# Two attention and SwiGLU layers in split fp32: which queue issues the first loads and the values' copies, the order of the normalization, of the transposes and of a product's parts, and which engine makes the weights' low parts

## The chip, the cores and the metric

The kernel runs on one core of one Trainium2 chip. The time is the device time of the slowest core, here the only one, in microseconds (us); the median of several runs counts. The engines of the core have these names in what follows: TensorE (PE in the profile; PEld is its weight load), VectorE (DVE), ScalarE (ACT), GpSimd (POOL) and SyncE (SP). SyncE computes nothing here; it only issues DMA copies. Each engine works through its own instructions in the order in which the program has them, and copies that an engine issues stand in that same order.

## What is computed

The input x has 2048 rows and 448 columns. All is in 32-bit floating point.

```python
def _A_ref(x, wq, wk, wv, wo):            # 16 heads of 28, one shared key and value head
    q = (x @ wq).reshape(B, S, H, Dh).transpose(0, 2, 1, 3)
    k = x @ wk
    v = x @ wv
    scores = jnp.einsum("bhqd,bkd->bhqk", q, k) * (Dh ** -0.5)
    p = _softmax(scores, axis=-1)
    o = jnp.einsum("bhqk,bkd->bhqd", p, v)
    return o.transpose(0, 2, 1, 3).reshape(B, S, H * Dh) @ wo

def _B_ref(x, w_gate, w_up, w_down):      # inner width 1792
    return (_silu(x @ w_gate) * (x @ w_up)) @ w_down

x = x + _A_ref(_layernorm(x), ...)
x = x + _B_ref(_layernorm(x), ...)
x = x + _A_ref(_layernorm(x), ...)
x = x + _B_ref(_layernorm(x), ...)
```

## The kernel before

**Number format.** TensorE takes its operands in a reduced form of fp32 (fp32r). A value is therefore held as a high part and a low part, both fp32r, and a product is high times high, high times low and low times high. A weight's high part is a cast (`wh`) and its low part the difference (`wl`); the normalized x has the parts `xh` and `xl`.

**Tiling.** The 2048 rows are four chunks c = 0 to 3 of 512 rows, each of four tiles of 128. The attention's projection of a chunk has four blocks of 128 output columns, written q(c,m) here. They are made in the order of `TURN`, m = 3, 0, 1, 2: block 3 holds the last 64 columns of q, then v and k; blocks 0 to 2 hold the other columns of q. A block is one `product_T` (L258): 11 matmuls of 128x512, for each of the four pieces k of 128 input columns. The fourth piece has only 64 columns, and its low part lies in the lower half of `xh[3]`, so it needs two matmuls where the others need three.

**What stands ahead of a chunk's blocks.** `norm_steps` (L211) gives the steps of the normalization: the statistics of four tiles on VectorE (L217, L218), `rstd` of all four on GpSimd (L222, L223), and for each tile the subtraction and scaling on VectorE (L230) and a copy of its last columns on GpSimd (L231). `flip` (L242) then turns the result: for each k four transposes on TensorE into one of the four banks `LOW` (L248), the high part by ScalarE (L252) and the low part by VectorE (L254, for k = 3 L256). The flip of chunk c+1 stands in `project` (L402) ahead of the last block of chunk c, that is of q(c,2).

**What a block leaves.** `q` (L422) empties the block's bank with ScalarE, for m = 3 and for the very first blocks straight into the high part (L439), otherwise as fp32 (L442), which GpSimd then splits (L140, L141). Both parts go into one of a ring of three buffers (`halves`, named q2) and from there by a copy to DRAM, `qd` (L445). A buffer is taken again only when its copy has landed. Block 3 also sends k into the stack of the keys `kstack` (four copies, issued by L132), and transposes v on VectorE (L454) and copies it into `vsb` (four copies, L456). `stack(i)` (L314) reads `qd` back into the stack of queries of a group of four heads, in four copies, `high(i)` (L323) reads the high parts alone into `qhigh`, and `diagonal` (four copies, L132) fills `kdiag`. With these two, `quick_steps` computes a bound for the softmax, which goes into the stack by four copies named `down` (L132). A list `waiting` lets one of diagonal, high and stack out behind each block.

**The queues.** All copies of the program are issued by SyncE, in program order. The framework gives every copy one of eight semaphores, in turn over all copies of the program, whichever queue they are on; a copy is not issued before the previous one on its semaphore has landed.

**The start.** The prelude (L731 to L764) issues the loads of the four tiles of chunk 0, then the first layer's weights (`load_wqkv`, L171: block 3's columns with v and k, then the first 256 of q), then the rows of chunks 1 to 3. ScalarE casts the first weights and VectorE makes their low parts (L193, L194; `parts`). GpSimd sets `kstack`, `vsb`, `qhigh`, `kdiag` and the three `qstack` to zero (from L747 to L759) and makes chunk 1's `rstd` behind them. `plan` says behind which block the normalization of the chunks 1 to 3 runs in layer 0. In layer 1 the normalized chunks come out of the feed-forward of layer 0 and `plan` is not used for them.

**Behind the projections.** The scores (L511), the exponentials (L518), the product with the values (L546), the output projection (L503), and the feed-forward (its products by `product_T`, L641 for the way down) take nearly all of the time. A second, slower form of the whole (`full`) stands behind a condition and isn't run on these inputs. The feed-forward uses `product_T` as well, and the order of its eleven matmuls is the same there.

## Time and profile before

| what | us |
|---|---|
| three runs | 2102.55, 2101.77, 2100.86 |
| their median | 2101.77 |
| profiled execution, its own time | 2104.14 |
| its span, first to last instruction | 2102.1 |

The stretches of the profiled execution, by busy time in us; the granted TensorE clock is a share of full speed, and the DMA share that of the core's 16 DMA engines:

| stretch (us) | what runs | TensorE | VectorE | ScalarE | GpSimd | clock | DMA share |
|---|---|---|---|---|---|---|---|
| 0 to 100 | start, projections of layer 0, first scores | 74.80 of 100 | 41.66 | 38.60 | 41.88 | 0.93 | 0.57 |
| 100 to 1016 | scores and feed-forward of layer 0 | 915.73 of 916 | 231.45 | 546.88 | 149.87 | 1.00 | 0.16 |
| 1016 to 1130 | projections of layer 1 | 100.42 of 114 | 51.81 | 33.94 | 31.68 | 0.94 | 0.36 |
| 1130 to 2102 | scores and feed-forward of layer 1 | 963.07 of 972 | 248.92 | 561.72 | 142.12 | 1.00 | 0.15 |

How the rows below are read. A row of a timeline has the start in us, the duration in us, the engine and the line of the program, the operation, the output and input by their names in the program, how many such instructions stand together, and in square brackets the idle time of that engine ahead of it with what ended it. SPq is SyncE's queue; its rows are issues of copies, and a row's duration there runs from the first issue of the group to the last's end. A row of waits has the engine's line, then what it waited for, then the total in us, how often, and the longest. A row of a grouped view has the operation with its shapes, then busy us in total and mean ns of one, then the idle time before. "LN <- DMA x" is a wait for the landing of a copy into x.

### The profile page before, as it was taken

The numbers are of one execution on the slowest core, as the hardware profiler recorded it, in microseconds if no ns is written. First come the engines' busy times: TensorE is split into PE (matmuls) and PEld (weight loads), VectorE is DVE, ScalarE is ACT, GpSimd is POOL, SyncE is SP. The second block draws the span as 40 slices with busy tenths as digits, with TensorE's granted clock in tenths as the row PEclk, the third lists the DMA queues.
The fourth block names the chain that finished last, engine by engine and source line by source line (L and its number), as shares of the span: only waits on it lengthen the run. The fifth ranks groups of instructions, "written<-read, shape, count | busy, mean of one in ns | idle before, by whom it ended". The sixth has DMA issues, their size and how long they took to land.

```text
span 2102.1 us, 28049 instructions
## 1 busy us (share of the span) xinstructions
PE 2054.0 (98%) x11073; PEld 1371.4 (65%) x11073; DVE 573.8 (27%) x1150; ACT 1181.1 (56%) x1600; POOL 365.5 (17%) x386
## 2 busy tenths in 40 slices
PE   7899999999999999999989999999999999999998
PEld 5544544545458888888775445455454588888887
DVE  6110131211105333333551112212111163333333
ACT  2599799798982111111127997988979621111111
POOL 5202010103201111111231111011212111111100
PEclk9999999999999999999999999999999999999999
DMA  6413122122200111110142222121322000111001
GB/s 183 137 30 70 30 54 49 35 53 60 49 6 20 29 29 29 29 29 10 32 130 79 55 51 50 29 56 29 70 43 48 25 10 21 29 29 30 29 1 72
DMA packets 98540, 97.21 MB, mean 46 GB/s; under 512 B 28992, under 2 KB 68320, under 8 KB 98400
## 3 DMA queue, kind: packets, MB, share of 16 engines
q1 hardware_dynamic: 98400, 95.34, 18.3%
q8 instruction: 89, 1.46, 0.3%
q14 instruction: 51, 0.42, 0.1%
HBM read 73.53 MB, written 18.61 MB: 44 GB/s over the span
## 4 chain that ended last, share of the span: by engine, by line
PE 91%; DMA 3%; DVE 2%; SPq 2%; POOL 1%; ACT 1%; issue 0%; ACTq 0%; POOLq 0%; DVEq 0%
PE bank L266 27%; PE bank L546 22%; PE pair L511 16%; PE bank L641 12%; PE bank L511 7%; PE pair L503 3%; DMA qd<-q 1%; PE pair L338 1%; PE bank L503 1%; DMA o<-rd 1%; PE bank L248 1%; DVE stats L217 1%; DVE xres L647 0%; SPq L132 0%; SPq L456 0%
## 5 line engine op out<-in xcount | busy, mean ns | idle before, releaser
L518 ACT ACTIVATE pt<-pair 128x1024 f32<-128x1024 f32 x768 | 763.5, 1029 | 0.7 <-PE pair L511 0.7
L546 PE MATMUL bank<-pt,vsb 128*32 128x512 f32 x4096 | 492.1, 598 | 0.0
L511 PE MATMUL pair<-qstack,kstack 128*128 128x512 f32 x1536 | 399.7, 395 | 1.2 <-ACT q L442 1.2
L518 ACT ACTIVATE pt<-bank 128x512 f32<-128x512 f32 x512 | 308.2, 602 | 90.8 <-PE bank L511 84.2
L266 PE MATMUL bank<-xh,wgh 128*128 128x512 f32 x896 | 349.1, 390 | 0.3
L266 PE MATMUL bank<-xh,wgl 128*128 128x512 f32 x896 | 348.5, 389 | 0.0
L511 PEld LDWEIGHTS pair<-qstack,kstack 128*128 128x128 f32 x1536 | 286.4, 188 | 62.3 <-ACT q L442 2.1
L695 ACT ACTIVATE sg<-bank 128x512 f32<-128x512 f32 x112 | 67.2, 600 | 372.4 <-PE bank L266 358.6
L641 PE MATMUL bank<-wdh,h 128*128 128x448 f32 x896 | 273.0, 365 | 0.0
L546 PEld LDWEIGHTS bank<-pt,vsb 128*32 128x32 f32 x4096 | 107.2, 109 | 245.0 <-issue 243.9
L266 PE MATMUL bank<-xl,wgh 128*128 128x512 f32 x672 | 261.5, 389 | 0.0
L697 ACT CAST h<-sg 128x512 fp32r<-128x512 f32 x112 | 69.5, 620 | 319.9 <-DVE sg L696 319.9
L511 PE MATMUL bank<-qstack,kstack 128*128 128x512 f32 x512 | 218.8, 427 | 2.7 <-ACT pt L518 2.7
L511 PEld LDWEIGHTS bank<-qstack,kstack 128*128 128x128 f32 x512 | 96.0, 187 | 156.1 <-ACT pt L518 144.4
L579 POOL TENSOR_TENSOR o<-o 128x512 f32<-128x512 f32 x32 | 41.2, 1287 | 898.7 <-DMA o<-rd 712.3
L266 PEld LDWEIGHTS bank<-xh,wgl 128*128 128x128 f32 x896 | 168.2, 188 | 35.0
L266 PEld LDWEIGHTS bank<-xh,wgh 128*128 128x128 f32 x896 | 168.2, 188 | 34.8 <-issue 1.7
L696 DVE TENSOR_TENSOR sg<-bank,sg 128x512 f32<-128x512 f32 x112 | 77.5, 692 | 414.9 <-PE bank L266 398.8
L641 PEld LDWEIGHTS bank<-wdh,h 128*128 128x128 f32 x896 | 168.1, 188 | 14.8
L641 PE MATMUL bank<-wdl,h 128*128 128x448 f32 x448 | 162.5, 363 | 0.0
L558 DVE COPY o<-bank 128x512 f32<-128x512 f32 x32 | 22.1, 692 | 456.1 <-PE bank L546 456.1
L266 PEld LDWEIGHTS bank<-xl,wgh 128*128 128x128 f32 x672 | 126.1, 188 | 23.5
(98 smaller groups left out, 1507.7 us busy)
## 6 DMA issues: line engine op xcount, KB each, us to landing
qstack<-qd SPq DMA_DIRECT2D x128, 224.0 KB
qd<-q SPq DMA_DIRECT2D x24, 512.0 KB
o<-rd SPq DMA_DIRECT2D x32, 256.0 KB
qhigh<-qd SPq DMA_DIRECT2D x128, 56.0 KB
wdr<-in_B_w_down_dram SPq DMA_DIRECT2D x28, 224.0 KB
wr<-in_B_w_gate_dram SPq DMA_DIRECT2D x28, 192.0 KB
wr<-in_B_w_up_dram SPq DMA_DIRECT2D x28, 192.0 KB
out_dram<-xres SPq DMA_DIRECT2D x16, 224.0 KB
```

The source lines that it names most:

```text
L217: nc.vector.bn_stats(stats[:, 4 * c + t, :], xres[:, 4 * c + t, :])
L266: nc.tensor.matmul(po, a, b, start=(i == 0), stop=(i == len(seq) - 1))
L503: nc.tensor.matmul(po[:, 0:D], a[:, g, ts_], b[:, g, :], start=(g + z == 0), stop=(g == NG - 1 and z == 2))
L511: nc.tensor.matmul(sp[:, e, :], kt_[:, P * kt : P * kt + P], qts[i % 3][:, j, :], start=True, stop=True)
L518: nc.scalar.activation(pt[:, 0 : len(which), :], sp[:, 0 : len(which), :], AF.Exp, scale=SCALE)
L546: nc.tensor.matmul(accs[i][32 * j : 32 * j + 32, :], vsb[:, kt, :], pts.pop((i, (kt, j))), start=(kt == 0), stop=(kt == NT - 1), skip_grou ...
L558: nc.vector.tensor_copy(oraw, accs.pop(i))
L579: nc.gpsimd.tensor_tensor(rb, oraw, rb, ALU.mult)
L641: nc.tensor.matmul(po, a[:, ts_], b, start=(fc == fs[0] and z == 0), stop=(fc == fs[-1] and z == 2))
L695: nc.scalar.activation(sg, pg[0], AF.Silu)
L696: nc.vector.tensor_tensor(sg, pg[1], sg, ALU.mult)
L697: nc.scalar.copy(hh, sg)
```

## The change

- The first layer's loads of wv, wk and the first 256 columns of wq are issued by ScalarE's queue; the remaining columns of wq stay on SyncE (`rows3` takes the engine).
- The subtraction that gives the first weights' low parts runs on GpSimd. The second pair of weight parts is made ahead of the memsets of `kdiag`, `qhigh` and `qstack`, not behind them, and the identity matrix is made ahead of the weights' loads.
- Normalization: chunk 0's `rstd` is made in two halves, the first as soon as the statistics of two tiles are there. The statistics and `rstd` of chunk 1 run in the prelude, and its scaling behind the first block. The statistics of chunks 2 and 3 come one block later than before, their scaling where it was (`plan`). The loads of chunks 1 to 3 are issued ahead of chunk 0's statistics.
- `flip` takes its four banks first, and issues the 16 transposes so that tiles 0 and 1 of all four k come first, then tiles 2 and 3; the copies and subtractions follow all transposes.
- `product_T` multiplies the four high-by-high pairs first, then three high-by-low pairs, then four low-by-high pairs. This holds for the feed-forward too.
- The copies of the values into `vsb` are issued by ScalarE's queue, after the next block's bank has been emptied (`later`), not by SyncE behind the keys. `diagonal` enters `waiting` a little earlier in the same block and is issued by ScalarE in layer 0.

```diff
-    def rows3(dst, src):
+    def rows3(dst, src, eng=None):
         n = src.shape[1]
-        nc.sync.dma_start(dst[:, 0:3], src[0:384, :].rearrange("(k p) n -> p k n", p=P))
-        nc.sync.dma_start(dst[:, 3], src[384:448, :][None].to_broadcast([2, 64, n]))
+        eng = eng or nc.sync
+        eng.dma_start(dst[:, 0:3], src[0:384, :].rearrange("(k p) n -> p k n", p=P))
+        eng.dma_start(dst[:, 3], src[384:448, :][None].to_broadcast([2, 64, n]))
...
-                rows3(r[:, :, 192 : 192 + DH], wv)
-                rows3(r[:, :, 224 : 224 + DH], wk)
+                rows3(r[:, :, 192 : 192 + DH], wv, nc.scalar if first else None)
+                rows3(r[:, :, 224 : 224 + DH], wk, nc.scalar if first else None)
             else:
-                rows3(r, wq[:, 0:256])
+                rows3(r, wq[:, 0:256], nc.scalar if first else None)
...
-                nc.vector.tensor_tensor(wl[:, :, zs], r, wh[:, :, zs], ALU.subtract)
+                nc.gpsimd.tensor_tensor(wl[:, :, zs], r, wh[:, :, zs], ALU.subtract)
...
-        def scale():
+        def scale(ts=slice(0, 4)):
...
+        if c == 0:
+            fs = [lambda t=t: stat(t) for t in range(4)]
+            fs[1:2] = [fs[1], lambda: scale(slice(0, 2))]
+            fs += [lambda: scale(slice(2, 4))] + [lambda t=t: apply(t) for t in range(4)]
+            got["first"] = fs
...
-        for k in ks:
-            pt = place if place is not None else bank(LOW)[1]
-            for t in range(4):
-                nc.tensor.transpose(pt[:, P * t : P * t + P], got["x"][:, t, P * k : P * k + P], ident)
+        pts = {k: place if place is not None else bank(LOW)[1] for k in ks}
+        order = [(k, t) for k in ks for t in range(4)]
+        if len(pts) == 4:
+            order.sort(key=lambda o: o[1] // 2)
+        for k, t in order:
+            nc.tensor.transpose(pts[k][:, P * t : P * t + P], got["x"][:, t, P * k : P * k + P], ident)
+        for k, pt in pts.items():
...
-        for k in range(3):
-            seq += [(a_h[k], xh[:, k, :]), (a_h[k], xl[:, k, :]), (a_l[k], xh[:, k, :])]
-        seq += [(a_h[3], xh[:, 3, :]), (a_l[3], xh[:, 3, :])]
+        for a, b, n in ((a_h, xh, 4), (a_h, xl, 3), (a_l, xh, 4)):
+            seq += [(a[k], b[:, k, :]) for k in range(n)]
...
         def diagonal(self):
             for j in range(4):
-                dma(kd[32 * j : 32 * j + DH, j, :], kt_[0:DH, 0:64])
+                eng = nc.sync if self.layer else nc.scalar
+                eng.dma_start(kd[32 * j : 32 * j + DH, j, :].bitcast(F32), kt_[0:DH, 0:64].bitcast(F32))
...
+            while self.later:
+                self.values(*self.later.pop())
...
-            for u in range(4):
-                nc.sync.dma_start(
+            self.later.append((c, vt))
+
+        def values(self, c, vt):
+            for u in range(4):
+                nc.scalar.dma_start(
...
-    fs, got = norm_steps(0)
-    for f in fs[:4]:
-        f()
+    make_identity(nc, ident)
     parts, at.w = load_wqkv(xb.enter_context(tc.tile_pool(name="wqkv0", bufs=1)), True)
-    make_identity(nc, ident)
-    for f in fs[4:]:
-        f()
-    at.norms[0] = got
...
+    _, got = norm_steps(0)
+    for f in got["first"]:
+        f()
     parts[0]()
-    at.turned(0)
+    flip(got, at.X[0])
...
-    for t in [*qms, *([kd] if kd is not None else []), *qts]:
+    parts[1]()
+    for t in [*([kd] if kd is not None else []), *qms, *qts]:
         nc.gpsimd.memset(t.bitcast(F32), 0.0)
-    parts[1]()
     for c in range(1, NC):
         fs, got = norm_steps(c)
-        at.plan.setdefault((max(0, 4 * c - 6), 1), []).extend(fs[:5])
-        at.plan[4 * c - 3 - (c > 1), 1] = fs[5:] + [lambda c=c, got=got: at.norms.__setitem__(c, got)]
+        if c == 1:
+            for f in fs[:5]:
+                f()
+            at.plan[0, 1] = fs[5:]
+        else:
+            at.plan[4 * c - 5, 1] = fs[:5]
+            at.plan[4 * c - 4, 1] = fs[5:]
+        at.norms[c] = got
```

More of the change, by code (lines that the diff above doesn't have):

```diff
@@ L213, in norm_steps @@
         got = {}
-        cs = slice(4 * c, 4 * c + 4)
         def stat(t):
@@ L218, in stat @@
             nc.vector.bn_aggr(mv[:, 4 * c + t, :], stats[:, 4 * c + t, :])
-        def scale():
-            rstd = pers.tile([P, 4], F32, name="rstd", bufs=2)
-            nc.gpsimd.tensor_scalar(rstd, mv[:, cs, 1], 1.0, EPS, ALU.mult, ALU.add)
-            nc.gpsimd.tensor_tensor(rstd, rstd, halfn, ALU.pow)
-            got["r"] = rstd
+        def scale(ts=slice(0, 4)):
+            if "r" not in got:
+                got["r"] = pers.tile([P, 4], F32, name="rstd", bufs=2)
+            v = mv[:, 4 * c + ts.start : 4 * c + ts.stop, 1]
+            nc.gpsimd.tensor_scalar(got["r"][:, ts], v, 1.0, EPS, ALU.mult, ALU.add)
+            nc.gpsimd.tensor_tensor(got["r"][:, ts], got["r"][:, ts], halfn[:, ts], ALU.pow)
         def apply(t):
@@ L279, in __init__ @@
             self.order = [(c, m) for c in range(NC) for m in TURN]
-            self.seen = 0
+            self.seen, self.later = 0, []
             self.steps, self.places = [], []
@@ L449, in q @@
                 return
+            if c == 0 and not full:
+                self.waiting.append(self.diagonal)
             for z in range(2):
@@ L459, in q @@
                 )
-            if c == 0 and not full:
-                self.waiting.append(self.diagonal)
         def open(self):
```

## The prediction, made before the changed kernel ran

> **What bounds the kernel now.** I read the page first, then TensorE's waits, then the chain of waits and SyncE's queue in the two stretches where TensorE waits.

> ```profile
> span 2102.1 us, 28049 instructions
> PE 2054.0 (98%) x11073; PEld 1371.4 (65%) x11073; DVE 573.8 (27%) x1150; ACT 1181.1 (56%) x1600; POOL 365.5 (17%) x386
> ...
> PE bank L248 <- ACT q L442: 15.2, 4, 5.2
> PE bank L248 <- DVE xn L230: 13.6, 3, 9.9
> ```

> TensorE is busy 98%, so almost nothing can be won or lost in scores and feed-forward. Its idle time (us in total, times, longest) lies in the projections: 15.2 us before transposes (L248) whose bank ScalarE has not yet emptied, 13.6 before transposes whose x is not yet normalized (9.9 of it the start). The change works on just these. The chain through the first projections shows what the 15.2 us are:

> ```profile
> 51.63 6.99 DMA qd<-q
> ...
> 58.72 0.59 ACT q L442
> ...
> 60.01 4.74 DMA qd<-q
> ...
> 78.51 2.14 DMA kstack<-q
> ```

> The copy qd(1,1) left SyncE at 51.63 and landed at 58.62; that freed the buffer into which ScalarE empties q(2,0). qd(1,2) left at 60.01 and landed at 64.75, which freed q(2,1)'s. The last two banks of flip(3) wait for these. So this stretch runs at the pace at which SyncE gets qd(1,1) and qd(1,2) out. The queue, and what it waits for:

> ```profile
> 44.15 2.70 SPq L456 DMA_DIRECT2D vsb<-sg  x4
> 46.89 1.90 SPq L323 DMA_DIRECT2D qhigh<-qd  x4
> ...
> 49.33 2.21 SPq L314 DMA_DIRECT2D qstack<-qd  x4
> 51.63 0.38 SPq L445 DMA_DIRECT2D qd<-q  x1
> 52.07 2.98 SPq L314 DMA_DIRECT2D qstack<-qd  x4
> 55.58 3.55 SPq L132 DMA_DIRECT2D qstack<-down  x4
> 60.01 2.01 SPq L445 DMA_DIRECT2D qd<-q  x2
> ...
> SPq L445 <- DMA qstack<-qd: 1.7, 2, 0.9
> ```

> The last row is the key to this change: qd(1,2), whose data is ready, waits 0.9 us for an unrelated copy, the first of stack 2. The two share a semaphore: eight go round over all copies, and a copy is issued only when the last one on its semaphore has landed.

> **Part 1: the start, +2.1 us.** Two subtractions of 128x1024 leave VectorE (1.23) for GpSimd, ahead of memsets and of chunk 1's rstd.

> ```profile
> 17.53 1.23 DVE L194 TENSOR_TENSOR wl<-wq,wh 128x1024 fp32r<-128x1024 f32 x1 [0.88 <-ACT wh L193]
> ...
> 11.83 1.04 ACT L193 CAST wh<-wr 128x1024 fp32r<-128x1024 f32 x1 [9.62 <-DMA wr<-in_A_wk_dram]
> 34.26 0.59 ACT L442 COPY q<-bank 128x512 f32<-128x512 f32 x1 [5.29 <-PE bank L266]
> ...
> L141 POOL TENSOR_TENSOR wl<-wr,wh 128x1024 fp32r<-128x1024 f32 x2 | 4.8, 2397 | 0.2
> ...
> 11.35 1.81 POOL L751 MEMSET kstack<- 128x2048 f32 x1
> 13.86 0.99 POOL L759 MEMSET qhigh<- 128x512 f32 x2
> 15.05 5.31 POOL L759 MEMSET qstack<- 128x2048 f32 x3
> 23.38 0.20 POOL L222 TENSOR_SCALAR rstd<-mv 128x4 f32<-128x4 f32 x1 [3.02 <-DVE mv L218]
> 23.66 1.02 POOL L223 TENSOR_TENSOR rstd<-rstd,halfn 128x4 f32<-128x4 f32 x1
> 24.71 1.78 DVE L230 TENSOR_SCALAR xn<-xres,mv,rstd 128x448 f32<-128x448 f32 x4 [0.70 <-POOL rstd L223]
> 25.28 2.91 PE L248 MATMUL bank<-ident,xn 128*128 128x128 f32 x16 [1.64 <-DVE xn L230]
> 30.06 0.50 PE L266 MATMUL bank<-xh,wh 128*128 128x512 f32 x1 [1.87 <-DVE xl L254]
> ```

> I leave the first weight cast at 11.83: its loads leave earlier on ScalarE, but each waits for a piece of x on its semaphore, and the last (wq's tail) for all of chunk 1 of x, with the cast behind it on the queue. GpSimd then runs without a gap: cast end 12.87, subtraction 2.40 to 15.3, memsets of kstack to vsb (11.35 to 13.86) 2.51 to 17.8, second subtraction to 20.2, the other memsets (13.86 to 20.36) 6.50 to 26.7, rstd (23.38 to 24.68) 1.30 to 28.0. VectorE normalizes chunk 1 until 29.8 (24.71 before). Behind that stands q(0,0)'s low part, 0.69, to 30.5; its bank is the third of flip(1), and in the new order 12 of the 16 transposes come behind it. At the slow pace of 0.27 (below; TensorE idles some 4 us) they end at 33.8, where q(0,2) starts instead of 30.06. That product ran at half clock (30.06 to 34.26); now at 11 x 0.23 = 2.5 it ends at 36.3: +2.1. Bounds: -1.9 (loads landing two us earlier, transposes at 0.12) to +4 (loads two us later). Hidden under this: the kdiag and values copies on ScalarE that hold q(0,1)'s emptying, and chunk 0's earlier normalization; without that cover flip(1)'s last bank would wait for them until about 28.

> **Part 2: SyncE up to qd(1,1), -0.5 us in each layer.** The values' four copies, 2.70 us (44.15), go to ScalarE. Counted from the end of q(0,2) (34.26), qd(1,1) left at 17.4. Now, by the built program's semaphores: qd(0,2) leaves at 2.7; stack 0's last copy waits until that has landed (4.74, to 7.45); qd(1,3) waits for stack 0's first, about 7.9, where the old one went at 5.5; then kstack 3.56, qhigh 1.90, qd(1,0), stack 1 2.21: qd(1,1) at about 16.9. Of 2.70 some 2.2 are lost to landings. Bounds -2.7 (no wait binds) to +2.

> **Part 3: qd(1,2) behind the values of chunk 2, +4.75 us in each layer.** Now qd(1,2) shares its semaphore with the third values copy of chunk 2, and the second and third "down" copies, ahead of it on SyncE, with the first two. These leave ScalarE only after it has emptied q(2,0), which itself waits for qd(1,1). From that landing: emptying 0.69, first copy's issue 0.68, landing 2.14 (taken from kstack's row, likewise SBUF to SBUF) = 3.5; three down copies at 0.89 = 6.15; then qd(1,2). Before, it left 60.01 - 58.62 = 1.4 after it. Difference 4.75, all of it TensorE's idle time before flip(3)'s last bank. Layer 1 has the same chain:

> ```profile
> 1090.39 0.39 SPq L445 DMA_DIRECT2D qd<-q  x1
> 1090.82 3.06 SPq L314 DMA_DIRECT2D qstack<-qd  x4
> ...
> 1098.59 1.64 SPq L445 DMA_DIRECT2D qd<-q  x2
> 1103.90 1.09 PE L248 MATMUL bank<-ident,xn 128*128 128x128 f32 x4 [5.25 <-ACT q L442]
> ```

> The landing of the small copies under load is not in the trace: 1.2 gives +3.8, qd's loaded 6.99 gives +9.6; I take 2.14, the nearest kind. [...]

> **Part 4: the transposes' order, +0.7 us in each layer.** Of flip(3) only the last 4 transposes came after the wait; sorted by pairs of tiles it is 10.

> ```profile
> 41.78 1.91 PE L248 MATMUL bank<-ident,xn 128*128 128x128 f32 x16
> 65.58 1.09 PE L248 MATMUL bank<-ident,xn 128*128 128x128 f32 x4 [5.10 <-ACT q L442]
> ```

> 1.91/16 is 0.12, after a long idle 1.09/4 is 0.27. [...]

> **Part 5: the hand-over to the scores, +1.15 and +1.45 us.** The last kstack copy of (3,3), which frees q(3,2)'s buffer, now waits for qd(3,3)'s landing.

> ```profile
> 80.24 0.39 PE L511 MATMUL bank<-qstack,kstack 128*128 128x512 f32 x1
> 81.39 0.97 PE L511 MATMUL pair<-qstack,kstack 128*128 128x512 f32 x3 [0.76 <-ACT q L442]
> ...
> 1119.86 0.39 PE L511 MATMUL bank<-qstack,kstack 128*128 128x512 f32 x1
> 1120.70 1.67 PE L511 MATMUL pair<-qstack,kstack 128*128 128x512 f32 x6 [0.45 <-ACT q L442]
> ```

> From q(3,3)'s end: qd after 1.4, landed +4.74, copy 0.86, landed +2.14, emptying 0.65: 9.8. Before, the pair ran 8.65 (layer 0) and 8.35 (layer 1) after that end (the pair at 81.39 and 1120.70; q(3,3) ended three products of 2.5 ahead of the first scores, 80.24 and 1119.86). Bounds 0 to 2.

> **Part 6: high parts first, +1.1 us in layer 1.** The fourth matmul now needs xh[3], whose lower half VectorE writes last.

> ```profile
> 1025.22 0.50 PE L266 MATMUL bank<-xh,wh 128*128 128x512 f32 x1 [0.94 <-DVE xl L254]
> ...
> 1026.40 0.69 DVE L256 TENSOR_TENSOR xh<-bank,xh 64x512 fp32r<-64x512 f32 x1
> ```

> It runs at 1027.12, eight more at 0.23 end the product's turn at 1028.9 instead of 1027.8. Bounds 0 to 1.2. In layer 0 the same wait lies under part 1. All other products follow work on TensorE that covers the flip, so their order costs nothing; with that cover gone each would pay this 1.1. The 2.70 us of copies also hold ScalarE before q(1,1), whose bank is flip(2)'s last: about 1.2 us of TensorE, covered by the later stall. Moved statistics of chunks 2 and 3 lie beside products.

> **Sum.** Layer 0: 2.1 - 0.5 + 4.75 + 0.7 + 1.15 = 8.2. Layer 1: 1.1 - 0.5 + 4.75 + 0.7 + 1.45 = 7.5. Together 15.7. The profiled execution took 2104.14 (span 2102.1 and 2.0 around it), 2.4 over the median of the runs: 2119.8 on that, 2117.5 on the median 2101.77.

> **Rivals.** *The shared semaphores never bind*: values land before SyncE comes to their successors. Then parts 3 and 5 fall away and part 2 is -2.7: 2.1 + 1.1 - 5.4 + 1.4 = -0.8, 2101.0. For it: 2.70 us is real issue time on a queue without gaps from 36.97 to 55. Against: the 0.9 us row. 15%.
> *Faster*: the start gains too, if chunk 1's rstd leaves GpSimd before 24.7, the point from which it decides. Then flip(1)'s waits (1.64, 1.87) and the half clock behind them (1.7) go, with 2.70 in each layer: -10.6, 2091.2. For it: VectorE is relieved of two subtractions and of chunk 2's statistics at that place. Against: GpSimd's 16 us of work behind the cast. 18%. [...]
> *Slower still*: the small copies queue behind stack 2 and land 2.7 us later in each layer: 2122.9. For it: DMA engines full in that stretch. 10%.

> **Numbers.** The forecast has 57%, its own range 2110 to 2124. The range 2093 to 2124 reaches past the first rival to the fast one with its half clock left (2091.2 + 1.7) and leaves out the rest of that one and what lies above the slowest. 0.2% (4.2 us) is about what a measurement of this kernel tells from no change: faster (under 2097.6) 0.18, same 0.17 (the first rival and the forecast's low end), slower 0.65.

> **What would show it.** Right: the wait before flip(3)'s last bank about 10 us instead of 5.1, with qd(1,2) issued about 6 us after qd(1,1) landed, SyncE waiting for vsb copies; chunk 1's rstd near 28; q(0,2)'s emptying near 36. Wrong: qd(1,2) out within 2 us of that landing, flip(1) begun before 26, or the scores beginning before 81.

## The result, and the profile after

The changed kernel took 2129.93 us (median of 4 runs, 2129.32 to 2131.34); the kernel before took 2102.16 beside it. The ratio is 1.0132 with a 95% interval of 1.0115 to 1.0150: 28 us slower. The prediction said slower, but 2117.5, and its range ended at 2124. The profiled execution took 2131.34.

The page of the changed kernel, and the waits of its TensorE (line, what ended the wait, total in us, how often, longest):

```profile
span 2129.5 us, 28037 instructions
PE 2060.0 (97%) x11073; PEld 1375.0 (65%) x11073; DVE 563.4 (26%) x1148; ACT 1181.7 (55%) x1600; POOL 370.4 (17%) x390
```

```profile
PE bank L256 <- ACT q L451: 23.9, 5, 8.9
PE bank L274 <- DVE xl L263: 13.6, 7, 9.0
PE bank L256 <- DVE xn L231: 12.3, 3, 8.0
PE bank L274 <- DVE xh L265: 3.1, 4, 1.0
PE bank L256 <- DVE sg L710: 2.9, 6, 0.7
```

The products' row of the kernel before:

```profile
PE bank L266 <- DVE xl L254: 4.3, 4, 1.9
```

L256 is the transpose (L248 before), L274 the product (L266), L451 the emptying (L442). Transposes behind an emptying waited 15.2 us before and wait 23.9 now. Products behind a flip waited 4.3 and wait 13.6; 9.0 of this is the very first product, since ScalarE copies the first flip (from 19.52) only behind the first weight cast (18.57). The last two rows are new. L265 is the low half of xh[3], which the fourth matmul now needs. L710 is a step of the feed-forward; there TensorE did not wait ahead of a transpose before.

The chain of waits through the first projections (start in us, duration, what):

```profile
6.68 11.71 DMA wr<-in_A_wk_dram
...
18.57 1.05 ACT wh L194
...
33.50 0.21 POOL rstd L224
...
62.09 7.44 DMA qd<-q
...
69.72 4.63 DMA vsb<-sg
...
76.08 2.84 DMA qd<-q
...
97.33 0.75 PE pair L525 x2
```

Read from the top: the last piece of wk landed at 18.39, and only then was the first weight cast (11.83 before). Chunk 1's rstd came at 33.50 (23.38). qd(1,1) left at 62.09 (51.63), and qd(1,2) at 76.08 (60.01), with a copy of the values between them. The first pair of scores started at 97.33 (81.39).

By stretches, each from one event to the next, in both traces:

| stretch | before | after | difference | forecast |
|---|---|---|---|---|
| start to the emptying of q(0,2) | 34.26 | 43.68 | +9.4 | +2.1 |
| to the first pair of scores | 47.13 | 53.65 | +6.5 | +6.1 |
| scores and feed-forward of layer 0, to the first product of layer 1's projections | 943.83 | 948.39 | +4.6 | 0 |
| layer 1's projections, to its first pair of scores | 95.48 | 99.94 | +4.5 | +7.5 |
| scores and feed-forward of layer 1, to the last transpose | 974.31 | 976.99 | +2.7 | 0 |
| sum | 2095.01 | 2122.65 | +27.6 | +15.7 |

### The profile page after: what moved, and what is told of

It is laid out like the page before. It is cut to its first block, busy times and chain, and to the rows that moved or that the text cites. A ratio compares the mean times of both kernels' runs of the same rounds, so it can differ in the third digit from the quotient of the medians.

```text
span 2129.5 us, 28037 instructions
## 1 busy us (share of the span) xinstructions
PE 2060.0 (97%) x11073; PEld 1375.0 (65%) x11073; DVE 563.4 (26%) x1148; ACT 1181.7 (55%) x1600; POOL 370.4 (17%) x390
## 4 chain that ended last, share of the span: by engine, by line
PE 91%; DMA 3%; DVE 2%; POOL 1%; SPq 1%; ACT 1%; issue 0%; ACTq 0%; DVEq 0%; POOLq 0%
PE bank L274 28%; PE bank L560 22%; PE pair L525 17%; PE bank L655 12%; PE bank L525 7%; PE pair L517 3%; PE pair L347 1%; DMA qd<-q 1%; PE bank L517 1%; DMA vsb<-sg 1%; PE bank L256 1%; DMA wr<-in_A_wk_dram 1%; DVE xl L263 0%; SPq L132 0%; DMA o<-rd 0%
## 5 line engine op out<-in xcount | busy, mean ns | idle before, releaser
L274 PE MATMUL bank<-xh,wgh 128*128 128x512 f32 x896 | 240.8, 390 | 3.5 <-DVE xh L265 1.9
L274 PE MATMUL bank<-xh,wgl 128*128 128x512 f32 x896 | 240.3, 390 | 0.0
L274 PEld LDWEIGHTS bank<-xh,wgh 128*128 128x128 f32 x896 | 168.2, 188 | 36.2 <-DVE xh L265 2.8
L274 PEld LDWEIGHTS bank<-xh,wgl 128*128 128x128 f32 x896 | 168.7, 188 | 35.2
L710 DVE TENSOR_TENSOR sg<-bank,sg 128x512 f32<-128x512 f32 x112 | 77.5, 692 | 425.4 <-PE bank L274 425.2
L274 PE MATMUL bank<-xl,wgh 128*128 128x512 f32 x672 | 189.3, 390 | 0.0
L655 PEld LDWEIGHTS bank<-wdh,h 128*128 128x128 f32 x896 | 168.2, 188 | 14.8
L274 PEld LDWEIGHTS bank<-xl,wgh 128*128 128x128 f32 x672 | 126.4, 188 | 26.3
```

The source lines that it names most:

```text
L274: nc.tensor.matmul(po, a, b, start=(i == 0), stop=(i == len(seq) - 1))
L655: nc.tensor.matmul(po, a[:, ts_], b, start=(fc == fs[0] and z == 0), stop=(fc == fs[-1] and z == 2))
L710: nc.vector.tensor_tensor(sg, pg[1], sg, ALU.mult)
```

## The experiments

Each time stands beside that of the kernel before in the same set of runs, whose median moved between 2100.5 and 2103.8 from one set to the next. What an edit of the changed kernel gave is told below as the difference of its median to 2129.9; since the sets differ, it is good to some 2 us. "Last wait" is TensorE's longest wait ahead of flip(3)'s last transposes, in layer 0 and layer 1; "scores" is the start of layer 0's first pair.

| run | what differs | us | before | ratio, 95% interval | last wait | scores |
|---|---|---|---|---|---|---|
| before | | 2102.2 | | | 5.10, 5.25 | 81.4 |
| after | the whole change | 2129.9 | 2102.2 | 1.0132, 1.0115 to 1.0150 | 8.79, 8.91 | 97.3 |
| e1_weights_sync | after, loads undone | 2121.4 | 2100.8 | 1.0092, 1.0076 to 1.0109 | 8.91, 9.36 | 89.3 |
| e2_values_sync | after, values undone | 2123.8 | 2100.8 | 1.0110, 1.0093 to 1.0126 | 5.74, 5.85 | 92.8 |
| e3_flip_old | after, transposes undone | 2122.0 | 2100.8 | 1.0097, 1.0080 to 1.0114 | 8.71, 8.82 | 94.1 |
| e4_product_old | after, product undone | 2122.1 | 2100.8 | 1.0103, 1.0087 to 1.0120 | 8.81, 8.36 | 96.7 |
| e5_four_undone | after, these four undone | 2103.8 | 2100.5 | 1.0014, 1.0005 to 1.0024 | 5.31, 4.55 | 83.4 |
| e6_chunks_later | after, x's last chunks later | 2124.0 | 2100.5 | 1.0107, 1.0089 to 1.0125 | 9.05, 9.11 | 91.7 |
| e7_values_now | after, values earlier on ScalarE | 2124.8 | 2100.5 | 1.0113, 1.0095 to 1.0131 | 7.43, 7.75 | 93.0 |
| e8_flip_product_old | after, transposes and product undone | 2115.1 | 2100.5 | 1.0061, 1.0043 to 1.0079 | 8.28, 8.84 | 94.2 |
| f1_values | before, values moved | 2109.4 | 2102.8 | 1.0029, 1.0020 to 1.0038 | 8.34, 8.79 | 86.3 |
| f2_flip_product | before, transposes and product changed | 2113.6 | 2102.8 | 1.0056, 1.0040 to 1.0071 | 5.56, 5.72 | 81.0 |
| f3_stacks_later | before, stacks later | 2105.0 | 2102.8 | 1.0007, 0.9998 to 1.0016 | none | 78.8 |
| f5_weights | before, loads moved | 2106.8 | 2102.8 | 1.0019, 1.0009 to 1.0028 | 5.25, 5.74 | 83.7 |
| g1_stacks_last | before, stacks behind the projections | 2086.6 | 2103.8 | 0.9918, 0.9902 to 0.9933 | none | 72.9 |
| g2_identity_later | after, the identity later | 2125.7 | 2103.8 | 1.0100, 1.0083 to 1.0117 | 8.96, 9.15 | 92.3 |
| g3_stacks_norm | g1 and the normalization's order | 2086.2 | 2103.8 | 0.9909, 0.9893 to 0.9926 | none | 71.3 |
| g4_values_sync_late | after, values on SyncE at the later place | 2124.8 | 2103.8 | 1.0098, 1.0081 to 1.0115 | 5.36, 6.17 | 92.9 |

### The start: whose loads come first

```diff
-                rows3(r[:, :, 192 : 192 + DH], wv, nc.scalar if first else None)
+                rows3(r[:, :, 192 : 192 + DH], wv)
```
(e1_weights_sync: so too for wk and wq's first columns.)

> The changed kernel with the first weights' loads back on SyncE, ahead of the loads of chunks 1 to 3 of x; all else as changed. Theory (the weights now share the DMA engines with 2.75 MB of x, which used to stand behind them): the first cast of weights moves from 18.6 to about 11.5 us, the first product from 20.9 to about 14, and the whole becomes 6 to 8 us shorter, 2122 to 2124. Rival (what counts at the start is GpSimd's chain up to chunk 1's rstd, with 13.9 us from the end of the cast to that rstd): the cast moves, but the rstd only by what the cast gives, and flip(1), now waiting for other things, gives back at least half: 3 us or less, about 2127.

The cast came at 10.85, the first product at 13.16, and 8.6 us were won on the changed kernel's median. The rival's half of the sum did not show.

```diff
-    for c in range(1, NC):
+    for c in range(1, 2):
         nc.sync.dma_start(xres[:, 4 * c : 4 * c + 4, :], xs[:, 4 * c : 4 * c + 4, :])
...
+    for c in range(2, NC):
+        nc.sync.dma_start(xres[:, 4 * c : 4 * c + 4, :], xs[:, 4 * c : 4 * c + 4, :])
     nc.gpsimd.memset(vsb, 0.0)
```
(e6_chunks_later)

> The changed kernel with the first weights' loads left on ScalarE, but with the loads of chunks 2 and 3 of x on SyncE behind the copies of ones, which wait for a memset of GpSimd; all else as changed. Theory (the weights land late because 2.75 MB of x go through the DMA engines beside them; now 0.9 MB): the first cast moves from 18.6 to 13 to 15 us, and the time falls by 3 to 6 us, to 2124 to 2127. Rival (ScalarE's queue itself, its issues one after the other and its waits on shared semaphores, makes the weights late): the cast stays over 17.5 and the time within 2 us of 2130.

The cast came at 13.51: with the same queue for the weights, the rows of x out of their way give back 5.1 us at this place and about 6 at the end. So it isn't ScalarE's queue as such.

The loads alone, on the kernel before (f5_weights, the first diff above turned round), should have cost the same:

> The kernel before with one part of the change alone: the first weights' loads of wv, wk and wq's first 256 columns on ScalarE's queue. Theory (SyncE then has the rows of chunks 1 to 3 out within some us, and 2.75 MB go through the DMA engines beside the weights): the first cast moves from 11.8 to 16 to 19 us, and the time rises by 5 to 9 us, to 2105 to 2109. Rival (the issues gain: the weights leave earlier on a queue of their own and the rest of the start has slack): the cast at 12 or earlier and no change of the time.

They did not: the first cast was at 12.75, only 0.9 later than before, the second at 19.56 (16.45 before), and the whole 4.0 us slower. Neither theory had the cast right. What else moved the loads in the changed kernel? ScalarE's queue in that kernel (start, us, engine, issue):

```profile
3.45 0.45 ACTq L137 DMA_DIRECT2D wr<-in_A_wv_dram  x1
3.94 1.15 ACTq L138 DMA_DIRECT2D wr<-in_A_wv_dram  x1
5.91 0.38 ACTq L137 DMA_DIRECT2D wr<-in_A_wk_dram  x1
6.68 1.67 ACTq L138 DMA_DIRECT2D wr<-in_A_wk_dram  x1
```

wv left at 3.45, in f5_weights at 1.14. Its load must stand behind the memset of the weights' pad (L183) on GpSimd (at 1.4 us here, at 0.8 in f5_weights), and the changed kernel makes the identity ahead of that memset. The fresh semaphores then go to SyncE's copies, two chunks of x among them, and in the built program wv's and wk's four loads each wait for one of the four tiles of chunk 0. One line moved back tells it:

```diff
-    make_identity(nc, ident)
     parts, at.w = load_wqkv(xb.enter_context(tc.tile_pool(name="wqkv0", bufs=1)), True)
+    make_identity(nc, ident)
```
(g2_identity_later)

> The changed kernel with one line moved back: the identity matrix is made behind the weights' loads. GpSimd then sets the weights' pad to zero first, and by the built program wv's loads leave first, on semaphores of their own, and SyncE's loads of chunks 1 to 3 wait for them. Theory (the order of issue and of the semaphores makes the weights late, not the queue that issues them): the first cast moves from 18.6 to 12 to 13.5 us, as with the loads alone in f5_weights (12.8), and the time falls by 4 to 7 us, to 2123 to 2126. Rival (the bytes of x beside them make the weights late in any order): the cast stays over 16 and the time within 2 us of 2130.

Its ScalarE queue:

```profile
1.14 0.47 ACTq L137 DMA_DIRECT2D wr<-in_A_wv_dram  x1
...
3.30 0.56 ACTq L138 DMA_DIRECT2D wr<-in_A_wk_dram  x1
...
11.87 1.05 ACT L194 CAST wh<-wr 128x1024 fp32r<-128x1024 f32 x1 [9.65 <-DMA wr<-in_A_wq_dram]
...
19.03 1.05 ACT L194 CAST wh<-wq 128x1024 fp32r<-128x1024 f32 x1 [4.17 <-DMA wq<-in_A_wq_dram]
```

wk's tail left at 3.30 instead of 6.68, and the first cast was at 11.87, where the prediction had left it; 4.2 us were won. So the order in which the copies take the eight semaphores decides the first cast: it put the weights behind tiles of x. That they then took so long to land (11.71 us for wk's tail) since the chunks 1 and 2 of x, issued at 3.81 and 4.27, went through the DMA engines ahead of them fits e6_chunks_later, but no run shows it alone: that edit takes chunk 2 away and also lets wv leave at 1.77, on a fresh semaphore. Nor is the first cast all that the loads cost. In g2_identity_later the second cast, at 19.03, is 3.1 later than with the loads on SyncE (15.97 in e1_weights_sync); GpSimd waits for it, chunk 1's rstd comes at 29.08 instead of 26.03, and the scores begin 3.1 later.

### The values: the place behind a waiting emptying

```diff
-            self.later.append((c, vt))
+            self.values(c, vt)
...
-                nc.scalar.dma_start(
+                nc.sync.dma_start(
                     vsb[32 * u : 32 * u + 32, 4 * c : 4 * c + 4, 0:DH],
```
(e2_values_sync)

> The changed kernel with the copies of the values back on SyncE at their old place; all else as changed. Theory (the copies of the values land 4.6 to 5.5 us after their issue and SyncE waits for them ahead of kstack and of the down copies): the wait ahead of flip(3)'s last transposes falls from 8.8 to about 5 us in both layers, qd(1,2) leaves about 9 us after qd(1,1) instead of 14, and the time falls by 8 to 12 us, to about 2120. Rival (the long wait belongs to the later start and the order of the transposes, the values' copies only show beside it): the wait stays over 7 us and the time falls by less than 3, since SyncE takes up 2.7 us of issuing in each layer.

The last wait fell to 5.74 and 5.85 and qd(1,2) left 8.2 us after qd(1,1) (61.74 and 69.93), as the theory had it; the time fell by 6.1, less than its 8 to 12.

Only the second hunk of it, so that the place in the program stays and the queue changes (g4_values_sync_late):

> The changed kernel with the values' copies issued by SyncE, but still at the later place, behind the next block's emptying in the program, so the semaphores go round as in the changed kernel. On SyncE the copies no longer wait for ScalarE's emptying, only for the transposing. Theory (the place behind a waiting emptying is what makes them late): the wait before flip(3)'s last transposes falls from 8.8 to 5 to 6.5 us and the time falls by 4 to 8 us, as with e2_values_sync (6.1). Rival (the later place itself and its semaphores are what costs): the wait stays over 8 us and the time within 2 us of 2130.

The last wait is 5.36 and 6.17, and 5.1 us are won. The semaphores go round as in the changed kernel, so they alone do not cost it. It is that on ScalarE the copies stand behind an emptying that waits for qd(1,1).

Only the first hunk, the values on ScalarE but a block earlier (e7_values_now):

> The changed kernel with the values' copies on ScalarE's queue, but at their old place in the program: right behind the transposing of the values, not behind the next block's emptying; all else as changed. By the semaphores the last copies of stack 2 and the first down copy then wait for the values of chunk 2, which leave a block earlier, and qd(1,2) waits for stack 2 as before the change. Theory (the long wait comes from where the values' copies stand in the order, behind an emptying that waits for qd(1,1)): qd(1,2) leaves about 10 us after qd(1,1) instead of 14, the wait before flip(3)'s last transposes is 5 to 6 us instead of 8.8, and the time falls by 5 to 8 us, to 2122 to 2125. Rival (any queue but SyncE's lets the small copies land 5 us late, and SyncE waits for them wherever they stand): the wait stays over 8 and the time within 2 us of 2130.

The time is as expected, the reason given for it is not: the last wait fell by only 1.4 and 1.2 us. Stack 2 now waits for the values (they left at 64.36 and landed at 68.76), and qd(1,2) stands behind it, 9.2 us after qd(1,1). The scores of layer 0 begin 4.3 earlier; a part of this is a first cast at 17.61, 1.0 earlier, which nothing in this edit explains.

The same part alone, on the kernel before (f1_values: `later` and `values` as in the change):

> The kernel before with one part of the change alone: the values' copies on ScalarE's queue behind the next block's emptying. By the built program's semaphores qd(1,2) then shares its semaphore with the third copy of the values of chunk 2, as in the changed kernel. Theory (the prediction's chain: landing of qd(1,1), emptying of q(2,0), values, down copies, qd(1,2)): qd(1,2) leaves 6 to 7 us after qd(1,1) has landed instead of 1.4, the wait before flip(3)'s last transposes goes from 5.1 to 8 to 9.5 us in each layer, and the time rises by 5 to 9 us, to 2106 to 2110. Rival (2.7 us of issuing leave SyncE, and the wait shows only because the rest of the changed kernel is late): the wait stays below 6 us and the time within 2 us of 2100.5 or below.

As the theory had it: 8.34 and 8.79, and 6.7 us slower. The chain of waits in that kernel:

```profile
52.90 6.14 DMA qd<-q
...
59.22 4.62 DMA vsb<-sg
63.85 0.53 SPq L132
...
65.58 2.83 DMA qd<-q
```

qd(1,1) landed at 59.04. The values left at 59.22, when ScalarE began to empty q(2,0), and landed at 63.84; three down copies of 0.5 later qd(1,2) left, 6.5 us after the landing. The prediction had 6.15 for this.

### The transposes and the product

```diff
-        pts = {k: place if place is not None else bank(LOW)[1] for k in ks}
-        order = [(k, t) for k in ks for t in range(4)]
-        if len(pts) == 4:
-            order.sort(key=lambda o: o[1] // 2)
...
+        for k in ks:
+            pt = place if place is not None else bank(LOW)[1]
+            for t in range(4):
```
(e3_flip_old)

> The changed kernel with the old order of the transposes (one bank at a time, its copies right behind it); all else as changed. Theory (copies that start only behind all 16 transposes hold the product behind the flip, whose bank is the flip's first, and taking four banks at once waits for a bank of the product ahead): the waits of 0.3 to 0.8 us ahead of and behind the flips of the feed-forward go (0.79, 0.64, 0.29 in each layer), with the slow clock behind them; 4 to 7 us less, about 2124. Rival (the order of the product alone makes these waits, through xh[3]): the waits on xh stay or grow to the same sum, and less than 2 us are won.

```diff
-        for a, b, n in ((a_h, xh, 4), (a_h, xl, 3), (a_l, xh, 4)):
-            seq += [(a[k], b[:, k, :]) for k in range(n)]
+        for k in range(3):
+            seq += [(a_h[k], xh[:, k, :]), (a_h[k], xl[:, k, :]), (a_l[k], xh[:, k, :])]
+        seq += [(a_h[3], xh[:, 3, :]), (a_l[3], xh[:, 3, :])]
```
(e4_product_old)

> The changed kernel with the old order of the eleven matmuls; all else as changed. Theory (the fourth matmul waits for xh[3], 0.95 us, four times where nothing covers the flip): these waits go, 3 to 4 us less, about 2126. Rival (the wait only changes its name, to the low part of the first pieces, since all copies stand behind the 16 transposes): about 1 us or less, 2129.

The first gave 8.0 us, a little more than expected, the second 7.9, twice what the theory had. TensorE in the first feed-forward, changed kernel (in brackets the idle time ahead and what ended it):

```profile
663.70 0.96 PE L274 MATMUL bank<-xh,wgh 128*128 128x512 f32 x3 [0.79 <-DVE xl L263]
665.62 0.50 PE L274 MATMUL bank<-xh,wgh 128*128 128x512 f32 x1 [0.96 <-DVE xh L265]
665.96 1.45 PE L274 MATMUL bank<-xl,wgh 128*128 128x512 f32 x3
667.20 1.91 PE L274 MATMUL bank<-xh,wgl 128*128 128x512 f32 x4
```

and the same place in the kernel before, where the product follows the flip without a wait:

```profile
645.74 1.25 PE L248 MATMUL bank<-ident,xn 128*128 128x128 f32 x10
647.13 0.50 PE L266 MATMUL bank<-xh,wgh 128*128 128x512 f32 x1
```

The wait of 0.79 goes with the old order of the transposes: the product's bank is the first that the flip used, and the last transpose into it is now the tenth, not the fourth. Its copy by ScalarE began 1.61 us after the first transpose (660.72 and 662.33), before the change 0.68 (645.09 and 645.77); not all 16 transposes are waited for, as I had thought. The 0.96 goes with the old order of the product. At this place there is only the second in e3_flip_old, only the first in e4_product_old. Behind both, the matmuls of the changed kernel come at some 0.43 us instead of 0.23 (four from 667.20 to 668.90; before, one from 647.47 to 647.71): the clock. Windows of 8.3 us from this product on, of the changed kernel and of e6_chunks_later, which has both waits as well (busy time of TensorE, its weight loads, VectorE, ScalarE and GpSimd, then clock, DMA share and GB/s):

```profile
663.70:672.00 8.30, 7.34 (x24) 5.60 (x25) 6.58 (x16) 1.29 (x3) 2.53 (x6) 0.79 0.00 0
```

```profile
658.48:666.78 8.30, 7.34 (x32) 5.96 (x33) 6.65 (x16) 1.28 (x3) 2.52 (x6) 1.00 0.00 1
```

The clock does not fall each time. Eight of the kernels (after, e1, e2, e6, e7, f2, g2, g4) have both waits close together at three such places each, and the window behind them is at 0.79 in 6 of the 24, at 1.00 in the rest. Where it falls in the changed kernel it is at half for 3.41 us, which costs some 1.7 us (an estimate, half of the 3.41); the other four windows show the same 0.79. In the changed kernel's profile it fell at two of its three places, in e4_product_old's at none; that is some 3.4 of the 10.2 us between these two profiled executions (2131.34 and 2121.14). By 6 in 24, an execution would have 0.75 such falls on average, 1.3 us (an estimate). Which places are hit stands in the last section.

> The changed kernel with the old order of the transposes and the old order of the eleven matmuls; all else as changed. Undoing the one gave 8.0 us, the other 7.9. Theory (each alone leaves one wait of 0.8 to 1 us, at which the clock stays full, and only both together bring the slow clock, so that each of the two already took back the same 2 us of slow clock in several places): together 10 to 13 us, 2117 to 2120, and no waits at all in the feed-forward. Rival (the two are independent): 16 us, 2114.

Both undone gave 14.8 us, between the two and nearer the rival's 16. Measured against the kernel before beside each run, it is 13.2 for both and 6.7 and 6.6 one by one, so the two add up within the error. What they would share, the slow clock, is by the estimate above smaller than these medians can tell. The feed-forwards had no such wait any more.

> The kernel before with the new order of the transposes and of the eleven matmuls, and nothing else of the change. Undoing both in the changed kernel gave 14.8 us. Theory (their cost is the waits behind the flips and the slow clock after two of them close together, in the feed-forward and the projections, whatever else is changed): 12 to 16 us slower than before, 2112 to 2117, with 4 to 5 us of it in the two feed-forwards. Rival (in the projections the new orders cost only since the start and the values are late as well): 5 to 8 us, of which all lies in the feed-forwards and at the begin of layer 1.

(f2_flip_product: the last two diffs turned round, on the kernel before.) 10.9 us by the medians and 8.2 between the events of the two profiles. By stretches the rival is right about the place: the scores of layer 0 began 0.4 earlier than in the kernel before, and the loss is +3.7 up to layer 1's first product, +2.2 in its projections and +2.7 behind them. By the size the runs lie between the two. In the profiled execution, the fastest of the four (2112.36 to 2116.22), the clock fell at none of the three places.

### What is left, and what the stall hid

> The changed kernel with four parts undone: the first weights' loads and the values' copies back on SyncE, the old order of the transposes and of the eleven matmuls. What is left of the change: normalization, weights' low parts on GpSimd, their place among the memsets, kdiag's copies on ScalarE in layer 0. Theory (these four carry the loss; what is left costs 2 to 3 us, since chunk 1's rstd still stands behind GpSimd's memsets and both low parts, so that flip(1) begins near 27 to 28 instead of 25.3): 2102 to 2105. Rival (the rest alone is a gain, VectorE being relieved: flip(1) by 25): under 2100. Other rival (the four do not add up, and the rest is worse still): over 2107.

2103.8, 3.2 us over the kernel before: the first theory. Chunk 1's rstd came at 26.43 (23.38 before) and flip(1) began at 28.33 (25.28), 3.05 later. This is the weights' low parts and the memsets on GpSimd ahead of it. The four parts undone together give 26.2 us; one by one they add up to 30.6. Against the kernel before beside each run these are 24.5 and 25.3: they add up within the error.

The long wait of both kernels is SyncE's way to qd(1,1) and qd(1,2). Two edits of the kernel before take the stacks out of it:

```diff
-            load = self.waiting.pop(0) if self.waiting else None
+            load = self.waiting.pop(0) if self.waiting and (full or self.seen in (1, 2, 7, 9, 10, 11)) else None
```
(f3_stacks_later)

> The kernel before, and no part of the change, but the copies that read the query stacks back go out later: stack 0 behind block (1,2) instead of (0,2), the second qhigh behind (2,0), stack 1 behind (2,1), stack 2 behind (2,2). The same copies, the same queue. Theory (the long wait of both kernels is SyncE's queue up to qd(1,1) and qd(1,2), in which the stacks stand with 7.7 us of issues that nobody needs before the scores): the waits before flip(3)'s last banks (1.95 and 5.10 us, 2.87 and 5.25) fall below 1 us each and the time by 8 to 15 us, to 2086 to 2093. Rival (the copies move the same bytes and the waits only move with them, to the last chunk or to the scores): the time within 3 us of 2100.5.

The waits ahead of flip(3) are gone, and the time is 2.3 us over the kernel before beside it, which the interval does not tell from no change: the rival. The chain of waits of that kernel names the new place:

```profile
65.85 8.01 DMA qstack<-qd
73.87 4.21 DMA kstack<-q
...
78.19 0.59 ACT q L442
78.82 2.93 PE pair L511 x6
```

The keys' copy of the last chunk stood behind stack 2 and held the last emptying; TensorE waited 10.55 us for it ahead of the scores, and 9.74 in layer 1.

```diff
+            load = self.waiting.pop(0) if self.waiting and (full or self.seen in (1, 2, 7, 9)) else None
...
+            while self.waiting:
+                self.waiting.pop(0)()
             self.advance(len(self.steps), NM + KC * LEAD if full else NM)
```
(g1_stacks_last)

> The kernel before, no part of the change: stack 0 goes out behind block (1,2), the second qhigh behind (2,0), and the stacks 1 and 2 behind the last block. The same copies on the same queue. In f3_stacks_later the waits before flip(3) went, but the first scores waited 10.6 us, because the last keys' copies stood behind stack 2. Theory (that wait came from stack 2 alone, issued at 65.9 us and landed 8.0 later): the wait before the scores is below 3 us in both layers, the scores begin 5 to 9 us earlier than before the change, and the time falls by 8 to 16 us, to 2085 to 2094. Rival (three buffers and the landing of qd set the pace of the last blocks, with or without stacks): the wait before the scores stays over 6 us and the time within 4 us of before.

Its TensorE ahead of the scores of both layers:

```profile
72.85 1.67 PE L513 MATMUL pair<-qstack,kstack 128*128 128x512 f32 x6 [2.76 <-ACT q L442]
...
1102.05 2.29 PE L513 MATMUL pair<-qstack,kstack 128*128 128x512 f32 x6 [1.77 <-ACT q L442]
```

2.76 and 1.77 us are left of the 10.55 and 9.74 of f3_stacks_later, the scores start 8.5 us earlier than before the change, and the kernel takes 2086.6: 0.8% faster than the kernel before, and faster than the changed one. With the change's order of the normalization added (g3_stacks_norm, weights' low parts on VectorE):

> g1_stacks_last with the change's order of the normalization of chunks 1 to 3 (statistics and rstd of chunk 1 in the prelude, its scaling behind the first block, the statistics of chunk 2 a block later), weights' low parts on VectorE as before. Theory (chunk 2's statistics stood on VectorE ahead of flip(1)'s low parts, and chunk 1's rstd waited for VectorE): flip(1)'s waits of 1.64 and 1.87 us fall below 1 us each, the slow clock behind them goes, and 2 to 5 us are won on g1_stacks_last. Rival (q(0,3)'s low part and its DMA, now behind four statistics on VectorE, make the next blocks as late): within 1 us of g1_stacks_last.

flip(1)'s two waits are gone and the scores begin at 71.28 instead of 72.85, but 2.0 us appear ahead of flip(2), and the whole is within 0.5 us. That is the rival's figure, though the cause that it gives isn't shown; the 1.6 us at the start are no more than these medians can tell.

## Why the prediction was right and wrong

**Part 1, the start: the step that failed.** "I leave the first weight cast at 11.83." It came 6.74 later. What the part built on it held: from the cast's start to chunk 1's rstd I had 26.7 - 11.83 = 14.9 us, and it took 33.50 - 18.57 = 14.9. The 2.1 forecast and the 6.7 of the cast make 8.8 of the 9.4 measured. That the 14.9 held is in part luck: with the first cast at 11.87 (g2_identity_later) the second one held GpSimd up, and the rstd came 17.2 us after the first, at 29.08. The late first cast hid this. I had seen that the loads would wait for tiles of x on their semaphores. I did not ask what those tiles and the chunks ahead of the weights do to their landing, and I did not see that the identity's move decides who takes a fresh semaphore (g2_identity_later). The bound of 2 us for later loads was too narrow.

**Part 2, SyncE up to qd(1,1): -0.5 forecast, +1.0 measured** (17.37 us from the emptying of q(0,2) before, 18.41 after). It lay within its bounds, but the sign was wrong: the copies of the keys of chunk 1 waited for the values on ScalarE to land (issued at 49.47, landed at 54.92), a wait that the part did not have.

**Part 3, qd(1,2) behind the values: right.** 6.15 us from the landing to qd(1,2) were forecast; it took 6.55 in the changed kernel and 6.5 with this part alone. Inside it the sizes were off and nearly cancelled, which is luck: the values took 4.63 from the start of their issue to the landing, where I had 0.68 + 2.14 (and the 2.14 of kstack's row holds its issue already); they left 0.19 after the landing of qd(1,1), not behind the emptying's 0.69; and the three down copies took 0.5 each, not 0.89. That the short landing would hold under load was my assumption; the runs show 4.63 and 4.62 (f1_values), so it was wrong here. qd(1,2) then landed in 2.84 instead of 4.74, so that the last wait was 8.8 and not the "about 10" of the forecast. That the whole stretch up to the scores came so near, +6.5 for +6.1, is luck too: part 2 was 1.5 over, and the way from qd(1,1)'s issue to flip(3)'s last transposes grew by 3.7, not by 4.75.

**Parts 4 and 5, to the scores.** From flip(3)'s last transposes to the first pair, 1.85 were forecast for layer 0 and 1.8 measured (15.81 and 17.58), but not as I had split them. The hand-over was no slower: the wait ahead of the pair is 0.49, and was 0.76; the last copy of the keys left 3.6 us after qd(3,3) (94.14 and 90.55), right behind the copy ahead of it, where I had let it wait for a landing of 4.74. In layer 1 the same stretch grew by 0.4 (16.80 and 17.24) where 2.15 had been forecast, which is most of why its +7.5 came out as +4.5. Part 5 was wrong, and that layer 0 agrees is luck. The mean clock of this stretch went from 0.90 to 0.83 in layer 0 and from 0.82 to 0.85 in layer 1: half clock lasted 2.8 us longer there and 0.7 less here. That is 1.4 of layer 0's 1.8 us (an estimate, half of the 2.8). No run shows part 4's 0.7: the ten transposes behind the wait took 2.37 us in both layers (at 79.75 and 1128.42), the four of the kernel before 1.09, which is 1.28 more.

**Part 6, the other step that failed.** "All other products follow work on TensorE that covers the flip, so their order costs nothing." In the feed-forward the product stands right behind its flip, 0.14 us behind it in the kernel before. The new orders made waits of 0.79 and 0.96 there, and up to 0.64 ahead of the later flips. With the slow clock in the first this is the 4.6 and 2.7 us of the two feed-forward stretches, for which I had nothing. I had read the absence of a wait as cover. It was only a good order. The same error stands at the start of the prediction: a TensorE that is busy 98% leaves little to win in the feed-forward, but not little to lose. In layer 1's first chunk, where I had the wait, it came (0.95 us), with 3.41 us of half clock behind it, which I had not.

**The rivals.** That the semaphores never bind is refuted (SyncE waits 6.0 us in all for landings of the values in layer 0's projections). The fast rival decided on chunk 1's rstd leaving GpSimd before 24.7; it left at 34.8.

So the direction and the longest chain were right. The size was wrong by about 12 us: 7.3 at the start, of which 6.7 are the landing of the first weights, and 7.3 in the feed-forwards, less 3.0 in layer 1's projections, more than half of it the hand-over that cost nothing.

## What to carry to other kernels

A copy moved to another queue takes its place in the order of everything on that queue: in f1_values the values left ScalarE at 59.22, behind an emptying that had waited for a landing at 59.04. Before moving it, ask what the instruction ahead of it waits for, and which copies behind it wait for its landing. When loads change queues, redo the start by bytes and by order: who leaves first, on which semaphore, and what goes through the DMA engines beside the load that is needed first. And a place without a wait is not a place with slack (the feed-forward's product stood 0.14 us behind its flip, and the new orders made waits of 0.79 and 0.96 there); look at the rows there, not only at the list of waits, before an order is changed for all users of a helper.

## What was not expected of the hardware

Which place is hit follows from this grid. Four cells of it in the changed kernel, at the first and at the last of its three places (busy time of the engines as above, then clock, DMA share and GB/s):

```profile
662.57:665.98 3.41, 1.66 (x9) 0.90 (x7) 2.97 (x5) 1.82 (x4) 0.00 (x0) 1.00 0.00 0
665.98:669.39 3.41, 3.41 (x10) 2.63 (x9) 2.50 (x8) 0.19 (x1) 0.60 (x2) 0.50 0.00 0
...
1710.45:1713.87 3.42, 2.57 (x18) 1.86 (x16) 2.01 (x4) 2.06 (x4) 0.00 (x0) 1.00 0.00 0
1713.87:1717.28 3.41, 2.45 (x12) 1.82 (x11) 3.25 (x9) 0.00 (x0) 0.00 (x0) 1.00 0.02 5
```

At the first place both waits lie in the cell that begins at 662.57: TensorE is busy for 1.66 us of it, and the next cell runs at half clock. At the last place the waits end at 1713.15 and 1715.07, the border at 1713.87 parts them, and the clock stays. So it is at all 24: at the 6 places 1.69 to 1.75 us of the two waits lie in one cell, at the 18 others at most 1.55. In the first feed-forward of e3_flip_old and of e4_product_old, with one of the two waits alone, the window behind it is at 1.00; in the 24 places the clock fell only where both waits lay in one cell. How much idle time it takes at other places isn't worked out here.
